# A token table laid out by partitions and read with one load, and both turned blocks of the first expert copied by ScalarE

## The chip, the cores and the metric

The kernel runs on one core of a Trainium2 chip. The metric is the device time of one execution in microseconds. A core has five engines that work side by side, each through its own list of instructions: PE (TensorE, matrix products), DVE (VectorE), ACT (ScalarE), POOL (GpSimd) and SP (SyncE, which here issues transfers only). Sixteen DMA engines move data between DRAM and the on-chip memory. Engines wait for one another and for transfers through semaphores.

## The reference, cut to what matters

Attention over 4 batches, 8 heads and 576 positions of 64 values, with a window in half of the heads and a dilated window in the others. Its result is read as 2304 tokens of 512 values. Each token then goes to one of 8 experts, the one with the largest gate value; an expert takes at most 576 tokens, in order:

```python
logits = x @ w_gate
expert_idx = np.argmax(logits, axis=1)
gate_w = probs[np.arange(N), expert_idx]
for i in range(N):
    e = expert_idx[i]
    if counts[e] < capacity:          # 576
        disp[e, counts[e]] = x[i]
        pos[i] = counts[e]
        counts[e] += 1
        keep[i] = True
h = np.maximum(np.einsum('ecd,edf->ecf', disp, w1), 0.0)
y = np.einsum('ecf,efd->ecd', h, w2)
out[i] = gate_w[i] * y[expert_idx[i], pos[i]]     # for kept tokens
```

## The kernel before, in words

**Attention and routing.** The 2304 tokens go through attention in nine stretches of 256 tokens (two blocks of 128). The kernel's builder holds a small planner (class `Plan`, line 64): every step is an operation with an engine, a duration, a rank and the operations it depends on, and the planner writes them out one by one, in the order in which they could start by its own durations. So each engine's list in this part is the planner's choice. A stretch loads its parts of q, k and v on SP's queue (lines 497 to 528), forms scores on PE, exponentials on ACT, row sums and their reciprocals on DVE (line 671), and multiplies the probabilities by those reciprocals on POOL (line 675: tiles `pr_7p` and so on, d and p for the two kinds of heads); PE transposes the result (line 681) and multiplies by v (line 703).

At the end of a stretch comes routing (`plan_route`, line 908). DVE takes the maximum of the gate values, the expert's number as `idx` (kept as e - 100) and a one-hot matrix; PE adds up ranks with a triangular matrix (line 993); DVE picks each token's rank within its expert, `rk` (line 1011), a large number `over_all` where the rank is 576 or more (line 1017), and the place in the table (lines 1021 and 1025), e * 576 + rank. Each of these is a DVE instruction on a 128 x 2 tile. The stretch's rows go to DRAM as `xrow` (issued by SP, line 848). Two scatters on POOL (line 1049), each with 128 entries of 4 bytes, write token numbers to the places in the DRAM tensor `table`, one 4-byte entry per place. The table starts filled with 2304 (lines 604, 757 and 773); that number stands for no token.

**Early work.** After the sixth stretch (number 5) the first two experts' lists are already partly known. `plan_early` (line 853) loads two blocks of 128 entries of both lists to `early_ix` (two loads, lines 859 to 865, issued by SP at line 863). They wait for that stretch's scatters, and later scatters wait for them. POOL then gathers the rows by those lists, two blocks for expert 0 and one for expert 1 (line 869), and SP's transposing transfers (line 884) turn them. Their products with w1 are among the last steps of attention.

**The experts.** After attention `load_index` (line 1153) brings all eight lists to the tile `ix`: eight loads of 4 x 128 entries (line 1159) and two for the last 64 entries, one for the first expert and one for the other seven (line 1161). Every entry is a 4-byte element of its own in the transfer, as neighbours of a list go to different partitions. POOL gathers the tokens' rows by these lists (line 1176): for the first expert its blocks 1, 2 and 0 in that order. A branch (line 1365) repeats early work where the early lists no longer hold. PE then multiplies expert 0's first block by w2 (`gemm2`, line 1273), and, as that expert's rows beyond the early ones came late, blocks 1 and 2 are turned on PE (`turn`, line 1197: eight 128 x 128 transposes at line 1202 into one bank each). The copy of the turned block from the bank to the tile `xe` alternates: ACT for block 1 (line 1207), DVE for block 2 (line 1205). `load_gate` and `second_gate` (DVE), `drain2` (ACT) and `base1`, the first products with `xe` (PE, line 382), follow. From the third expert on, SP's transfers turn the blocks instead. Weights of all experts come in 512-KB pieces (line 323), are split by ACT and DVE into a high and a low f16 part (`w1h`, `w1l`, `w2h`, `w2l`; lines 345 to 351), and results are scattered to the output by POOL (line 1277).

```python
def c_sl():
    nc.vector.scalar_tensor_tensor(out=small("sl", [128, NBK]), in0=flat("idx"), scalar=float(cap), in1=flat("rk"), ...)
def c_slots():
    nc.vector.scalar_tensor_tensor(out=slots[:, b0:b0 + NBK], in0=t["sl"], scalar=100.0 * cap, in1=over_all[:, b0:b0 + NBK], ...)
```

Of the kernel before, what the change touches and what calls it, by code (L numbers as in the profile page):

```python
# [13 lines left out]
I32 = mybir.dt.int32  # L14
AF = mybir.ActivationFunctionType
ALU = mybir.AluOpType
AX = mybir.AxisListType
# [23 lines left out]
NLIM = 6  # L41
# [163 lines left out]
def shape_constants(B, H, S, E, NT, cap):  # L205

    p = np.arange(128)
    parts = [np.eye(128, dtype=np.float32)]
    parts.append((p[:, None] < p[None, :]).astype(np.float32))
    parts.append(np.tile(np.arange(E, dtype=np.float32) - 100.0, (128, 1)))  # L210
    parts.append((np.arange(NT // 128)[None, :] * 128 + p[:, None]).astype(np.float32))
    for e in range(E):
        lims = form_limits(E, cap, e)
        parts.append(np.tile(np.array(lims + [1e9] * (NLIM - len(lims)), np.float32), (128, 1)))
    parts += unit_masks(B, S)[0]
    return np.ascontiguousarray(np.concatenate(parts, axis=1), np.float32)
# [3 lines left out]
def attention_moe(ctx: ExitStack, tc: tile.TileContext, q, k, v, w_gate, w1, w2, consts, out, cap):  # L220
# [25 lines left out]

    NC0 = 256 + E + NTB + E * NLIM
    con = cpool.tile([128, NC0], F32, name="con")
# [3 lines left out]
    tokid = con[:, 256 + E:256 + E + NTB]  # L252
    limits = con[0:1, 256 + E + NTB:NC0].rearrange("p (e k) -> p e k", e=E)
    tri = cpool.tile([128, 128], F16, name="tri")
# [9 lines left out]
    cnt_i = cpool.tile([1, E + 1], I32, name="cnt_i")  # L264
    nblk = (cap + 127) // 128
    blank = cpool.tile([128, RW], F32, name="blank")
# [5 lines left out]
    xrow = dpool.tile([NT + 1, RW], F32, name="xrow")  # L272
    table = dpool.tile([E * cap, 1], I32, name="table")

# [181 lines left out]
    with ExitStack() as actx:  # L456
# [146 lines left out]

        fill = ap1.tile([128, E * cap // 128], I32, name="fill")
        taken = {"S": 0, "T": 0, "V": 0}
# [247 lines left out]
        def plan_early(sb, at):  # L853
# [4 lines left out]

            def load(e):
                r = table[e * cap:(e + 1) * cap]  # L860
                full = sum(n == 128 for n in n_b)
                if full:
                    nc.sync.dma_start(out=lists[:, e, 0:full], in_=r[0:full * 128].rearrange("(a p) o -> p (a o)", p=128))
                if full < EB:
                    nc.sync.dma_start(out=lists[0:n_b[full], e, full:], in_=r[full * 128:cap])

# [7 lines left out]

            early_ix.extend(dma(lambda e0=e0: load(e0), 0.1, at + 0.6, sent[sb]) for e0 in range(len(EARLY)))
            for e0 in range(len(EARLY)):
# [4 lines left out]
                for j in range((EN[e0] + 127) // 128):  # L881
                    o = add(lambda e, e0=e0, j=j, g=g: fetch(e0, j, g), "POOL", 1.04, [clear, early_ix[e0], rows_out[sb]], at + 0.7, xfer=0.8)
                    n = n_b[j]
# [24 lines left out]
        def plan_route(sb, at):  # L908
# [107 lines left out]
            def c_over():  # L1016
                nc.vector.tensor_scalar(out=over_all[:, b0:b0 + NBK], in0=flat("rk"), scalar1=float(cap), scalar2=float(BIG),
                                        op0=ALU.is_ge, op1=ALU.mult)

            def c_sl():  # L1020
                nc.vector.scalar_tensor_tensor(out=small("sl", [128, NBK]), in0=flat("idx"), scalar=float(cap), in1=flat("rk"),
                                               op0=ALU.mult, op1=ALU.add)

            def c_slots():
                nc.vector.scalar_tensor_tensor(out=slots[:, b0:b0 + NBK], in0=t["sl"], scalar=100.0 * cap, in1=over_all[:, b0:b0 + NBK],
                                               op0=ALU.add, op1=ALU.add)

# [20 lines left out]
            def scatter(blk):  # L1048
                ins = nc.gpsimd.indirect_dma_start(  # L1049
                    out=table, out_offset=bass.IndirectOffsetOnAxis(ap=slots[:, blk:blk + 1], axis=0),  # L1050
                    in_=tok_i[:, blk:blk + 1], in_offset=None, bounds_check=E * cap - 1, oob_is_err=False)
                tc.declare_no_dep(ins.ins, group="dispatch", reason="slots are distinct")
# [7 lines left out]
            idx = dve(c_idx, [cand])  # L1060
            oh = dve(c_oh, [idx])
            rank = add(lambda e: c_rank(), "PE", 0.1, [oh, o_cast] + prev_seen, at + 0.3)
            sums = dve(c_sums, [ex])
# [12 lines left out]
            over = dve(c_over, [rk])  # L1076
            sl = dve(c_sl, [rk])
            slot = dve(c_slots, [over, sl])
            if last:
# [71 lines left out]
    nusual = min(BULK // 128, nblk)  # L1151

    def load_index(e0, e1):

        rows_e = table[e0 * cap:e1 * cap].rearrange("(e s) o -> s e o", s=cap)
        for e in range(e0, e1):
            r = table[e * cap:(e + 1) * cap]
            if nf:
                nc.sync.dma_start(out=ix[:, e, 0:nf], in_=r[0:nf * 128].rearrange("(a p) o -> p (a o)", p=128))
            if e == e0 and cap % 128:  # L1160
                nc.sync.dma_start(out=ix[0:cap % 128, e0:e1, nf], in_=rows_e[nf * 128:cap].rearrange("p e o -> p (e o)"))

# [171 lines left out]

    load_index(0, 1)
    if E > 1:
        load_index(1, E)
    gather(0)
# [43 lines left out]
    for e in range(min(E, len(EARLY))):  # L1382
        for i, j in enumerate(range(EN[e] // 128, nusual)):
            turn(e, j, banks[((3, 5), (6, 7))[e][i % 2]], (nc.scalar, nc.vector)[i % 2])
        if e == 0:
# [64 lines left out]
```

## Time and profile before

| what | us |
|---|---|
| three runs, median (lowest to highest) | 432.93 (431.42 to 433.8) |
| the profiled execution, its own time | 430.79 |
| its span, first to last instruction | 428.9 |
| PE busy | 341.7 (80%) |
| DVE busy | 244.9 (57%) |
| ACT busy | 228.5 (53%) |
| POOL busy | 147.9 (34%) |

The span is cut in 40 slices of 10.7 us; each digit is the busy share of an engine in tenths, PEclk the granted clock of TensorE in tenths of full speed, DMA the mean share in use of 16 engines:

| row | slices |
|---|---|
| PE | 5889957798792987667559899898958959899791 |
| DVE | 6799969997883748112152645643563475765200 |
| PEclk | 9999989999996999669699999999979999989898 |
| DMA | 7996898554798941559815299497695797990000 |

Attention ends near 165 us, in the sixteenth slice; the experts fill the rest. A releaser ("<-") is the instruction whose semaphore ended a wait, inferred from events; where the named engine had long been done, it was another. A stall counts only where the engine that bounds a stretch has to stand still for it.

### The profile page before, as it was taken

The numbers are of one execution on the slowest core, as the hardware profiler recorded it, in microseconds if no ns is written. First come the engines' busy times: TensorE is split into PE (matmuls) and PEld (weight loads), VectorE is DVE, ScalarE is ACT, GpSimd is POOL, SyncE is SP. The second block draws the span as 40 slices with busy tenths as digits, with TensorE's granted clock in tenths as the row PEclk, the third lists the DMA queues.
The fourth block names the chain that finished last, engine by engine and source line by source line (L and its number), as shares of the span: only waits on it lengthen the run. The fifth ranks groups of instructions, "written<-read, shape, count | busy, mean of one in ns | idle before, by whom it ended". The sixth has DMA issues, their size and how long they took to land. (4 is left out here: it accounts for less than half of the span.)

```text
span 428.9 us, 10118 instructions
## 1 busy us (share of the span) xinstructions
PE 341.7 (80%) x3643; PEld 245.7 (57%) x3643; DVE 244.9 (57%) x825; ACT 228.5 (53%) x577; POOL 147.9 (34%) x157
## 2 busy tenths in 40 slices
PE   5889957798792987667559899898958959899791
PEld 3677745475561777257544776774825637687340
DVE  6799969997883748112152645643563475765200
ACT  4888948687781871123161644553464375765210
POOL 6465756757425425532000230310301214110110
PEclk9999989999996999669699999999979989999898
DMA  7996898554798941559815299497695797990000
GB/s 209 252 241 188 166 269 213 134 150 83 87 106 314 156 168 54 101 137 352 111 60 215 85 234 280 157 204 268 215 195 216 243 235 260 174 303 29 29 32 29
DMA packets 83267, 74.59 MB, mean 174 GB/s; under 512 B 48098, under 2 KB 65506, under 8 KB 83187
## 3 DMA queue, kind: packets, MB, share of 16 engines
q1 hardware_dynamic: 78274, 61.23, 58.3%
q0 software_dynamic: 4912, 12.25, 8.2%
q8 instruction: 56, 0.92, 1.1%
q14 instruction: 25, 0.20, 0.2%
HBM read 58.09 MB, written 11.51 MB: 162 GB/s over the span
## 5 line engine op out<-in xcount | busy, mean ns | idle before, releaser
L382 PE MATMUL bank<-xe,w1h 128*128 128x192 f16 (+2 forms) x832 | 95.6, 241 | 18.2 <-issue 7.2
L382 PE MATMUL bank<-xe,w1l 128*128 128x192 f16 (+2 forms) x416 | 92.1, 241 | 0.0
L382 PEld LDWEIGHTS <-w1h 128*128 128x128 f16 x832 | 71.3, 100 | 22.8 <-ACT y L1290 9.5
L1277 POOL DMA_INDIRECT out_dram<-y,ix x26 | 26.5, 1021 | 163.9 <-ACT y L1284 138.6
L1273 PE MATMUL bank<-w2h,hh 128*128 128x512 f16 x120 | 47.9, 399 | 12.0 <-issue 8.9
L351 DVE SCALAR_TENSOR_TENSOR w1l<-wst,w1h 128x1024 f16<-128x1024 f32 x32 | 38.6, 1239 | 29.6 <-ACT w1h L345 28.5
L388 ACT ACTIVATE hh<-bank 128x384 f16<-128x384 f32 (+1 forms) x64 | 27.8, 476 | 40.0 <-PE bank L382 37.3
L389 DVE SCALAR_TENSOR_TENSOR hl<-bank,hh 128x384 f16<-128x384 f32 (+1 forms) x64 | 31.4, 534 | 30.7 <-ACT hh L388 24.1
L1273 PE MATMUL bank<-w2l,hh 128*128 128x512 f16 x120 | 47.9, 399 | 0.0
L1273 PEld LDWEIGHTS <-hh 128*128 128x128 f16 x240 | 23.9, 102 | 41.4 <-issue 16.0
L1273 PE MATMUL bank<-w2h,hl 128*128 128x512 f16 x120 | 47.4, 395 | 0.0
L1284 ACT ACTIVATE y<-bank,gate 64x512 f32<-64x512 f32 (+1 forms) x25 | 17.1, 684 | 55.4 <-PE bank L1273 30.1
L351 DVE SCALAR_TENSOR_TENSOR w2l<-wst,w2h 128x1024 f16<-128x1024 f32 x32 | 37.6, 1218 | 15.3 <-ACT w2h L345 11.2
L382 PEld LDWEIGHTS <-w1l 128*128 128x128 f16 x416 | 41.3, 100 | 0.2
L1291 DVE SCALAR_TENSOR_TENSOR y<-bank,gate,y 64x512 f32<-64x512 f32 x17 | 12.6, 743 | 44.9 <-ACT y L1290 43.4
L1176 POOL DMA_INDIRECT xg<-xrow,ix x26 | 26.3, 1011 | 33.4 <-DVE hl L389 21.0
L345 ACT ACTIVATE w2h<-wst 128x1024 f16<-128x1024 f32 x32 | 32.1, 1047 | 0.7
L1049 POOL DMA_INDIRECT table<-tok_i,slots x18 | 21.8, 1210 | 23.1 <-DVE lost_i L1037 6.6
L1290 ACT ACTIVATE y<-bank,gate 64x512 f32<-64x512 f32 x17 | 11.6, 684 | 31.3 <-PE bank L1273 24.8
L345 ACT ACTIVATE w1h<-wst 128x1024 f16<-128x1024 f32 x26 | 26.1, 1050 | 0.7
L725 DVE TENSOR_TENSOR xT<-bank,xT 128x128 f16<-128x128 f32 (+1 forms) x54 | 20.6, 448 | 4.4 <-ACT xT L535 4.1
L1273 PEld LDWEIGHTS <-hl 128*128 128x128 f16 x120 | 12.3, 102 | 15.7 <-issue 2.8
(350 smaller groups left out, 718.8 us busy)
## 6 DMA issues: line engine op xcount, KB each, us to landing
wst<-in_moe_w_dram SPq DMA_DIRECT2D x64, 512.0 KB
xrow<-row SPq DMA_DIRECT2D x9, 520.0 KB
vp<-in_v_dram SPq DMA_DIRECT2D x32, 96.0 KB
rawpq<-in_q_dram SPq DMA_DIRECT2D x6, 256.0 KB
rawpk<-in_k_dram SPq DMA_DIRECT2D x6, 256.0 KB
vd<-in_v_dram SPq DMA_DIRECT2D x4, 384.0 KB
vd<-in_v_dram SPq DMA_DIRECT2D x2, 320.0 KB
vd<-in_v_dram SPq DMA_DIRECT2D x2, 256.0 KB
```

The lines of the kernel that those rows point to most:

```text
L345: nc.scalar.activation(out=hi, in_=t, func=AF.Copy, scale=SW)
L351: nc.vector.scalar_tensor_tensor(out=lo, in0=t, scalar=SW, in1=hi, op0=ALU.mult, op1=ALU.subtract)
L382: nc.tensor.matmul(out=view(f), lhsT=w[wt][:, c, f * 128:(f + 1) * 128], rhs=x[:, xo + c, a:a + n], start=(kk == 0), stop=(kk == 3 * ND - 1))
L388: nc.scalar.activation(out=hh, in_=p, func=AF.Relu)
L389: nc.vector.scalar_tensor_tensor(out=hl, in0=p, scalar=0.0, in1=hh, op0=ALU.max, op1=ALU.subtract)
L725: nc.vector.tensor_tensor(out=dst, in0=src, in1=hi, op=ALU.subtract)
L1049: ins = nc.gpsimd.indirect_dma_start(out=table, out_offset=bass.IndirectOffsetOnAxis(ap=slots[:, blk:blk + 1], axis=0), in_=tok_i[:, blk:b ...
L1176: nc.gpsimd.indirect_dma_start(out=g[:n, j], out_offset=None, in_=xrow, in_offset=bass.IndirectOffsetOnAxis(ap=ix[:n, e, j:j + 1], axis=0) ...
L1273: nc.tensor.matmul(out=p[:n], lhsT=ht[:, f, j * 128:j * 128 + n], rhs=w[wt][:, f], start=first, stop=final)
L1277: ins = nc.gpsimd.indirect_dma_start(out=out, out_offset=bass.IndirectOffsetOnAxis(ap=ix[:n, e, j:j + 1], axis=0), in_=y[:n], in_offset=No ...
L1284: nc.scalar.activation(out=y[a:n], in_=bank2(e, j)[a:n], func=AF.Copy, scale=gate[a:n, e, j:j + 1])
L1291: nc.vector.scalar_tensor_tensor(out=y[0:m], in0=p[0:m], scalar=gate[0:m, e, j:j + 1], in1=t[0:m], op0=ALU.mult, op1=ALU.add)
```

## The change

It has four parts. The place of a token of rank r at expert e becomes row r mod 128, column e * 5 + r // 128 of a table of 128 rows and 40 columns, so the flat place is r * 40 + e * 5 + r // 128 - (r // 128) * 128 * 40. The number r // 128 is counted on DVE by comparing the rank with 128, 256, 384 and 512 (four new columns of the constants) and summing the ones. Two consecutive ranks of one expert are then 160 bytes apart instead of 4. The early lists of both experts become one load of 256 pieces of two neighbouring entries, the eight main lists one load of 128 rows of 160 bytes. And both turned blocks of expert 0 are copied by ACT; expert 1 keeps one block each for ACT and DVE. The routing of a stretch has four DVE instructions more (first, block, blocks, place), and `slots` is a plain sum.

```diff
+    parts.append(np.tile(128.0 * np.arange(1, (cap + 127) // 128, dtype=np.float32), (128, 1)))
...
-    table = dpool.tile([E * cap, 1], I32, name="table")
+    table = dpool.tile([128 * E * nblk, 1], I32, name="table")
+    by_place = table.rearrange("(p e a) o -> p e (a o)", p=128, e=E)
+    starts = con[:, NC1:NC0]
...
-        fill = ap1.tile([128, E * cap // 128], I32, name="fill")
+        fill = ap1.tile([128, E * nblk], I32, name="fill")
...
-            def load(e):
-                r = table[e * cap:(e + 1) * cap]
-                full = sum(n == 128 for n in n_b)
-                if full:
-                    nc.sync.dma_start(out=lists[:, e, 0:full], in_=r[0:full * 128].rearrange("(a p) o -> p (a o)", p=128))
-                if full < EB:
-                    nc.sync.dma_start(out=lists[0:n_b[full], e, full:], in_=r[full * 128:cap])
+            def load():
+                nc.sync.dma_start(out=lists, in_=by_place[:, 0:len(EARLY), 0:EB])
...
-            early_ix.extend(dma(lambda e0=e0: load(e0), 0.1, at + 0.6, sent[sb]) for e0 in range(len(EARLY)))
+            early_ix.append(dma(load, 0.1, at + 0.6, sent[sb]))
...
-                    o = add(lambda e, e0=e0, j=j, g=g: fetch(e0, j, g), "POOL", 1.04, [clear, early_ix[e0], rows_out[sb]], at + 0.7, xfer=0.8)
+                    o = add(lambda e, e0=e0, j=j, g=g: fetch(e0, j, g), "POOL", 1.04, [clear, early_ix[0], rows_out[sb]], at + 0.7, xfer=0.8)
...
+            def c_first():
+                nc.vector.tensor_scalar(out=small("first", [128, NBK]), in0=flat("idx"), scalar1=100.0, scalar2=float(nblk),
+                                        op0=ALU.add, op1=ALU.mult)
+            def c_block():
+                nc.vector.tensor_tensor(out=small("past", [128, NBK, nblk - 1]), in0=t["rk"].broadcast_to([128, NBK, nblk - 1]),
+                                        in1=starts.rearrange("p (a k) -> p a k", a=1).broadcast_to([128, NBK, nblk - 1]), op=ALU.is_ge)
+            def c_blocks():
+                nc.vector.tensor_reduce(out=small("blk", [128, NBK]), in_=t["past"], axis=AX.X, op=ALU.add)
             def c_sl():
-                nc.vector.scalar_tensor_tensor(out=small("sl", [128, NBK]), in0=flat("idx"), scalar=float(cap), in1=flat("rk"),
+                nc.vector.scalar_tensor_tensor(out=small("sl", [128, NBK]), in0=flat("rk"), scalar=float(E * nblk), in1=t["first"],
                                                op0=ALU.mult, op1=ALU.add)
+            def c_place():
+                nc.vector.scalar_tensor_tensor(out=small("place", [128, NBK]), in0=t["blk"], scalar=1.0 - 128 * E * nblk, in1=t["sl"],
+                                               op0=ALU.mult, op1=ALU.add)
             def c_slots():
-                nc.vector.scalar_tensor_tensor(out=slots[:, b0:b0 + NBK], in0=t["sl"], scalar=100.0 * cap, in1=over_all[:, b0:b0 + NBK],
-                                               op0=ALU.add, op1=ALU.add)
+                nc.vector.tensor_tensor(out=slots[:, b0:b0 + NBK], in0=t["place"], in1=over_all[:, b0:b0 + NBK], op=ALU.add)
...
-            sl = dve(c_sl, [rk])
-            slot = dve(c_slots, [over, sl])
+            blk = dve(c_blocks, [dve(c_block, [rk, o_con])])
+            sl = dve(c_sl, [rk, first])
+            slot = dve(c_slots, [over, dve(c_place, [sl, blk])])
...
-    load_index(0, 1)
-    if E > 1:
-        load_index(1, E)
+    nc.sync.dma_start(out=ix, in_=by_place)
...
-            turn(e, j, banks[((3, 5), (6, 7))[e][i % 2]], (nc.scalar, nc.vector)[i % 2])
+            turn(e, j, banks[((3, 5), (6, 7))[e][i % 2]], nc.scalar if e == 0 else (nc.scalar, nc.vector)[i % 2])
```

## Rows read from the trace of the kernel before

**Rows 1.** The page of the profile, part 1: busy time in us of each engine, its share of the span, and its number of instructions.

```profile
PE 341.7 (80%) x3643; PEld 245.7 (57%) x3643; DVE 244.9 (57%) x825; ACT 228.5 (53%) x577; POOL 147.9 (34%) x157
```

**Rows 2.** What TensorE waited for over the whole run: line waiting, the engine and tile that ended the wait, us in total, times, longest.

```profile
PE bank L681 <- POOL pr_7p L675: 8.5, 1, 8.5
...
PE bank L1273 <- ACT hh L438: 5.7, 1, 5.7
...
PE bank L681 <- POOL pr_3d L675: 4.3, 1, 4.3
PE bank L382 <- DVE xe L1205: 4.2, 1, 4.2
```

**Rows 3.** Busy time in us of each engine (and instructions) in the stretch from 61 to 130 us; then TensorE's granted clock, the share of the DMA engines and the GB/s they moved.

```profile
61.00:130.00 69.00, 56.80 (x767) 41.52 (x764) 62.68 (x347) 54.99 (x210) 38.50 (x40) 0.99 0.67 130
```

**Rows 4.** POOL's timeline between 40 and 186 us: start, duration in us, engine, line, operation, tiles, count; in brackets the idle time before it and what ended it.

```profile
41.51 0.97 POOL L1049 DMA_INDIRECT table<-tok_i,slots  x1 [0.30 <-issue]
...
57.07 1.26 POOL L545 TENSOR_TENSOR pairq<-rawpq,blank 128x512 f32<-128x512 f32 x1 [4.86 <-DVE w1l L351]
...
116.73 0.97 POOL L1049 DMA_INDIRECT table<-tok_i,slots  x1 [0.30 <-PE bank L939]
...
123.27 0.83 POOL L675 TENSOR_TENSOR pr_7d<-pr_7d,su_7d 128x384 f32<-128x384 f32 x1 [2.57 <-ACT pr_7p L655]
132.26 1.29 POOL L869 DMA_INDIRECT early_g<-xrow,early_ix  x1 [8.17 <-DMA early_ix<-table]
133.86 1.77 POOL L869 DMA_INDIRECT early_g<-xrow,early_ix  x1 [0.30 <-DVE mx_8p L647]
135.93 1.00 POOL L869 DMA_INDIRECT early_g<-xrow,early_ix  x1 [0.31 <-issue]
136.96 1.61 POOL L675 TENSOR_TENSOR pr_7p<-pr_7p,su_7p 128x384 f32<-128x384 f32 x2
...
164.35 4.71 POOL L1049 DMA_INDIRECT table<-tok_i,slots  x1 [0.30 <-issue]
175.39 1.04 POOL L1176 DMA_INDIRECT xg<-xrow,ix  x1 [6.33 <-DMA ix<-table]
```

**Rows 5.** What SP's DMA queue waited for over the whole run.

```profile
SPq L1159 <- DMA table<-tok_i,slots: 9.0, 1, 9.0
...
SPq L863 <- DMA table<-tok_i,slots: 4.4, 1, 4.4
```

**Rows 6.** SP's timeline, in stretches around 43, 125 and 172 us: start and duration of the issues of a line, the tiles, and how many issues.

```profile
42.76 3.63 SPq L497 DMA_DIRECT2D rawdk<-in_k_dram  x2
...
119.66 0.93 SPq L528 DMA_DIRECT2D vp<-in_v_dram  x2
125.08 0.90 SPq L863 DMA_DIRECT2D early_ix<-table  x2
126.03 2.44 SPq L323 DMA_DIRECT2D wst<-in_moe_w_dram  x3
...
171.77 0.36 SPq L1159 DMA_DIRECT2D ix<-table  x1
```

**Rows 7.** Stretches of 2 us: busy time in us of each engine (and instructions), TensorE's granted clock, the mean busy share of the DMA engines (over 1 where packets overlap), and GB/s.

```profile
14.00:16.00 2.00, 2.00 (x19) 1.19 (x19) 1.52 (x17) 2.00 (x13) 0.49 (x2) 1.00 0.91 202
42.00:44.00 2.00, 1.94 (x23) 1.45 (x20) 1.97 (x10) 1.40 (x4) 1.99 (x3) 1.00 1.06 84
44.00:46.00 2.00, 1.66 (x18) 1.20 (x16) 2.00 (x11) 2.00 (x10) 1.57 (x3) 1.00 0.53 21
120.00:122.00 2.00, 2.00 (x28) 1.31 (x28) 1.74 (x8) 2.00 (x13) 0.69 (x1) 1.00 1.89 63
122.00:124.00 2.00, 2.00 (x42) 1.51 (x36) 2.00 (x7) 2.00 (x8) 0.73 (x1) 1.00 0.90 15
124.00:126.00 2.00, 1.46 (x30) 1.21 (x28) 2.00 (x16) 0.90 (x5) 0.09 (x1) 1.00 0.47 25
132.00:134.00 2.00, 0.00 (x0) 0.00 (x0) 1.26 (x4) 0.00 (x0) 1.43 (x2) 0.50 1.02 409
134.00:136.00 2.00, 0.00 (x0) 0.00 (x0) 0.74 (x1) 0.00 (x0) 1.69 (x2) 0.50 0.98 388
```

**Rows 8.** VectorE's timeline at 128 us: the first and the last of four small operations that stand next to one another.

```profile
128.35 0.15 DVE L987 RECIPROCAL row<-sums 128x2 f32<-128x2 f32 x1
...
128.57 0.16 DVE L671 RECIPROCAL su_7p<-su_7p 128x4 f32<-128x4 f32 x1
```

**Rows 9.** The one line that holds the branch: its engines' instructions, duration in ns (least, median, most), and the start of the first and last in us.

```profile
L1365 PEldq COMPARE_BRANCH  x1: 5601/5601/5601, 169.2 to 169.2; - x1
```

**Rows 10.** VectorE's timeline at the end of attention and at the first expert's turn.

```profile
162.41 0.15 DVE L1021 SCALAR_TENSOR_TENSOR sl<-idx,rk 128x2 f32<-128x2 f32 x1
162.60 0.16 DVE L1025 SCALAR_TENSOR_TENSOR slots<-sl,over_all 128x2 int32<-128x2 f32 x1
...
186.90 0.69 DVE L1205 COPY xe<-bank 128x1024 f16<-128x1024 f16 x1 [10.08 <-remote]
```

**Rows 11.** TensorE's timeline at the first expert's turn: the transposes, and the first products behind them.

```profile
182.39 1.06 PE L1202 MATMUL bank<-ident,xg 128*128 128x128 f16 x16
187.64 0.50 PE L382 MATMUL bank<-xe,w1h 128*128 128x192 f16 x2 [4.20 <-DVE xe L1205]
```

**Rows 12.** ScalarE's timeline at the same place.

```profile
184.10 1.02 ACT L1207 ACTIVATE xe<-bank 128x1024 f16<-128x1024 f16 x1 [8.11 <-issue]
```

More of the change, by code (lines that the diff above doesn't have):

```diff
@@ L245, in attention_moe @@
     ctx.enter_context(tc.manual_schedule())
-    NC0 = 256 + E + NTB + E * NLIM
+    nblk = (cap + 127) // 128
+    NC1 = 256 + E + NTB + E * NLIM
+    NC0 = NC1 + nblk - 1
     con = cpool.tile([128, NC0], F32, name="con")
@@ L252, in attention_moe @@
     tokid = con[:, 256 + E:256 + E + NTB]
-    limits = con[0:1, 256 + E + NTB:NC0].rearrange("p (e k) -> p e k", e=E)
+    limits = con[0:1, 256 + E + NTB:NC1].rearrange("p (e k) -> p e k", e=E)
     tri = cpool.tile([128, 128], F16, name="tri")
@@ L264, in attention_moe @@
     cnt_i = cpool.tile([1, E + 1], I32, name="cnt_i")
-    nblk = (cap + 127) // 128
     blank = cpool.tile([128, RW], F32, name="blank")
@@ L1050, in scatter @@
                     out=table, out_offset=bass.IndirectOffsetOnAxis(ap=slots[:, blk:blk + 1], axis=0),
-                    in_=tok_i[:, blk:blk + 1], in_offset=None, bounds_check=E * cap - 1, oob_is_err=False)
+                    in_=tok_i[:, blk:blk + 1], in_offset=None, bounds_check=128 * E * nblk - 1, oob_is_err=False)
                 tc.declare_no_dep(ins.ins, group="dispatch", reason="slots are distinct")
@@ L1061, in plan_route @@
             oh = dve(c_oh, [idx])
+            first = dve(c_first, [idx])
             rank = add(lambda e: c_rank(), "PE", 0.1, [oh, o_cast] + prev_seen, at + 0.3)
@@ L1151, in attention_moe @@
     nusual = min(BULK // 128, nblk)
[L1153 to L1161, printed above, removed]
     def late_order(e):
```

## The prediction

> **What bounds the kernel now.** I read the page first. TensorE (PE) leads with 80% of the span, but VectorE (DVE) has 57% and neither share says which of them ends a stretch [rows 1]. So next came PE's waits. Four of them concern this change: 8.5 us for POOL's normalised probabilities pr_7p, 4.3 us for pr_3d, 5.7 us for ACT's hh at line 438, and 4.2 us for the turned block at line 1205 [rows 2]. The third view is busy time by stretch. Between 61 and 130 us DVE is busy 62.68 of 69.00 us and PE only 56.80: there DVE is the bound [rows 3]. Outside of it PE is held by single late arrivals.
>
> The longest arrival is the stop that ends at 137.84. POOL's timeline shows its chain. After 123.27 POOL stands until 132.26, put down to the load of the early lists; then three gathers follow, and only behind them, at 136.96, the normalisation that PE wants [rows 4]. SP's queue shows why the list came late. Its issue had waited 4.4 us for the table scatter [rows 5], went out at 125.08 in two pieces, and three weight loads followed from 126.03 [rows 6].
>
> The fourth view is what the DMA engines moved, in stretches of 2 us. Behind the pair of scatters whose second starts at 116.73 [rows 4] the rate falls to 63, 15 and 25 GB/s, while the engines' busy share goes as high as 1.89: they are occupied and move almost nothing. The same follows the pair whose second starts at 41.51 (84, then 21 GB/s). At 132 to 134 us, where gathers run but no scatter, it is 409. From 14 to 16 us, behind the write that fills the table with 144-byte rows, it is 202 [rows 7]. So the stall comes with the scatters, which write 128 single 4-byte entries each, and not with any write to the table.
>
> **The change part by part.**
>
> *Layout.* A token of rank r now goes to row r mod 128 of a row-per-partition table. Tokens that follow one another in an expert's list lay 4 bytes apart and now lie 160 bytes apart. The number of writes, their size and the 18 POOL instructions stay. What the distance is worth no row shows. One end is nothing, the other the whole of the stalls behind scatters. The first stall: PE stands 8.5 us before 137.84. If the scatters land at once, SP, done with its earlier issues at 120.59 (119.66 + 0.93 [rows 6]), can issue the list then. Taking the 3.6 us from list issue at 171.77 to the gather at 175.39 as landing [rows 4, 6], the gathers begin at 124.3. At the 1.00 us of the third one each, with two gaps of 0.3, they end by 127.9. The reciprocal that pr_7p needs starts at 128.57 [rows 8], so POOL is free in time and after 0.9 us of its normalising (137.84 less 136.96) PE goes on at about 129.6, 8.2 us earlier. DVE used the stop, though: 1.26 us in 132 to 134 and 0.74 in 134 to 136 [rows 7], weight work that must then be done elsewhere by the engine that bounds. I take 6.2.
>
> The second stall: SP's pair of loads at 42.76 took 3.63 us to issue, inside the stall [rows 6]; a pairq on POOL at 57.07 comes after 4.86 us of waiting [rows 4], and PE's wait for pr_3d follows it. The wait is named after DVE, whose own work was finished just then, so a late load is my reading, and I take 2 of its 4.3 us. The third is at attention's end: the last scatter occupies POOL for 4.71 us, and SP waits 9.0 us for it [rows 4, 5]. PE's branch at line 1365 takes 5.6 us [rows 9], and ACT's hh, behind which PE waits 5.7, comes after it. Whether a branch is held up by the DMA stall no row shows: between 0 and 5.6, and I take 1.5, nearer nothing, as it starts 5 us after the last scatter's issue. Together the layout gives 9.7, or nothing.
>
> *Four more DVE instructions in each of nine stretches* (first, block, blocks, place; slots only changes its kind). Small DVE operations that stand among others start 0.07 us apart: the four from 128.35 to 128.57 [rows 8]. For the 28 of the seven stretches that lie before the stop this is 28 x 0.073 = 2.0 us; DVE has 0.91 of its time in use there, so 1.9 count. Bounds are 0 (they fall into DVE's idle tenth) and 36 x 0.08 = 2.9. In the last stretch, where each one waits for the one before, they start 0.19 apart (162.41 to 162.60 [rows 10]). The way from rank to slots gets two links longer, +0.4 on the path, as scatters, lists and gathers all queue behind it.
>
> *The early list as one load* of 256 eight-byte pieces for two of 256 four-byte ones. Its issue shrinks from 0.90 us for both [rows 6] by half, and of the some 6.3 us between issue and gather up to half may go. In the case above it is already contained; without relief it is worth 0 to 3.1, and I take 1.5 (neither end is nearer by a row).
>
> *The main lists as one load* of 128 rows of 160 bytes in place of ten loads. The first goes out at 171.77 in 0.36 us [rows 6]; the nine behind it fall away. POOL's first gather could start perhaps 1.5 us before 175.39. I cost it at nothing: the gathered blocks are turned by PE only at 182.39, behind the pass that starts once hh is there [rows 11], so that pass covers the gathers. If the branch came sooner, the gather would be the next thing late, which is why I gave the third stall only 1.5.
>
> *The turned block.* ACT takes 1.02 us for a copy [rows 12], DVE 0.69 at 186.90 [rows 10]. If PE hands the second block over only then, ACT ends 0.33 later and PE at 187.64 [rows 11] starts as much later. If the block was ready when ACT finished the first at 185.12, ACT would end at 186.14 and not 187.59: 1.4 sooner. DVE did nothing else for 10 us, which speaks for the first; I take 0 between +0.3 and -1.4.
>
> *The filling write* grows from 144 to 160 bytes a row, hidden as it is now by 202 GB/s behind it [rows 7]. The bounds are numbers in instructions that are there anyway, and four more columns ride in the load of the constants, for which nothing in [rows 2] waits.
>
> **The sum.** -6.2 - 2.0 - 1.5 + 1.9 + 0.4 + 0 = -7.4. The profiled execution took 430.79 us, 428.9 of it the span, so it would go to 423.4. It lies 2.1 under the median of 432.93 on which I forecast: 432.93 - 7.4 = 425.5.
>
> **The rivals.** One half per cent, 2.2 us, is about what a measurement of this kernel can tell from no change.
>
> *A, the sum above.* For it speaks that the engines are busy and move nothing, and only where entries lying next to one another are written. Against it: entries of eight experts are mixed already, and a stall that begins 2 to 3 us after a scatter has left POOL might belong to something else that runs then. Its range goes from the whole stalls without the DVE debit (-8.2 - 4.3 - 1.5 + 1.9 + 0.4 - 1.4 = -13.1, 420) to a third of the 9.7 with DVE's additions hidden (-3.2 + 0.4 = -2.8, 430).
>
> *B, the stall is a price of each small write, wherever it goes.* The 256 writes of a pair remain, and so do the stalls; the new layout's only gain is the shorter early list. +1.9 + 0.4 - 1.5 + 0 = +0.8, 433.7, with 431.5 to 435. For it: both layouts write 4 bytes at a time, and the fill, whose rows are 36 times as long, passes without a stall, which fits size as well as distance. The Trainium skill says as much in "DMA: Bandwidth & Descriptors", Specifications: a transfer under 512 B makes the engine read, modify and write. The trace agrees for 4 bytes and not for 144; by that rule alone B would hold.
>
> *C, the slower one.* DVE bounds 61 to 130 and is given 36 more instructions, each a full turn of its queue; no stall goes, and the early list lands when the weight loads queued behind it let it. +2.9 + 0.4 + 0.3 = +3.6, 436.5. It decides as soon as the layout and the list together give less than 1.4 us.
>
> *That the change doesn't do what it says:* the planner may place the longer chain so that the gathers still go ahead of pr_7p. That falls under A when the list is early (it costs nothing then) and under B when it isn't.
>
> **How the numbers follow.** A 0.55, B 0.26, C 0.19. I prefer A because three separate stalls have the same sign (occupied engines, no bytes) and stand behind scatters alone; I keep almost half because nothing in the trace parts distance from count. The predicted time is A's, 425.5, by itself 420 to 430. The range reaches over B to the lower part of C: 421.0 to 435.5; left out are A's best end (0.04) and most of C (0.14). A is faster by over 0.5%, B within it, C slower: 0.55, 0.26, 0.19.
>
> **What would show it.** Right: in 120 to 126 us over 100 GB/s, the list issued by SP near 121, gathers near 124 and no PE wait over 2 us for pr_7p; the rate in 42 to 46 at 150 or more; one load of the main lists near 172 or before. DVE's small operations in 61 to 130 up by 20, its busy time there by 1.5 to 2. For B: 10 to 60 GB/s again behind each pair of scatters, and the gathers' wait only 1 to 3 us shorter. For C: PE's waits for DVE rows in 61 to 130 grow by 2 or more, and the stop at 130 stays. What would make it wrong altogether is a planned order in which other work moves: a wait of PE for a row that isn't in [rows 2].

## The result, and the profile after

The changed kernel took 421.06 us (median; four runs from 418.18 to 425.26) beside 432.46 for the kernel before. The ratio is 0.9713, with an interval of 0.9648 to 0.9777; ratios, here and below, take the undisturbed runs alone, medians all of them. The kernel is faster, as forecast, but by 11.4 us between the medians (12.4 by the ratio) where the sum said 7.4. On the forecast's scale the ratio gives 420.5, just under the range's lower end of 421.0.

The profiled execution after took 421.89 us, its span 420.1. The first view is busy time by stretch (busy us of each engine, granted clock, share of the DMA engines, GB/s), answering [rows 7].

```profile
42.00:44.00 2.00, 1.42 (x19) 0.93 (x18) 2.00 (x8) 1.43 (x3) 1.55 (x2) 1.00 0.76 177
44.00:46.00 2.00, 2.00 (x28) 1.42 (x28) 1.44 (x15) 1.78 (x6) 1.82 (x3) 1.00 1.09 312
120.00:122.00 2.00, 2.00 (x26) 1.67 (x26) 1.39 (x6) 2.00 (x12) 0.00 (x0) 0.50 0.36 87
122.00:124.00 2.00, 2.00 (x23) 1.48 (x20) 1.91 (x11) 1.52 (x8) 0.82 (x1) 0.89 0.94 218
124.00:126.00 2.00, 2.00 (x23) 1.30 (x23) 1.60 (x20) 1.98 (x7) 0.83 (x1) 1.00 0.82 271
```

Where the rate had been 63, 15 and 25 GB/s it is 87, 218 and 271, and from 44 to 46 it is 312 in place of 21. The 87 is no stall: the DMA engines' share is 0.36, so there was little to move, where before it was 1.89 at 63 GB/s. TensorE's granted clock reads 0.50 from 120 to 122, the lower of its two levels, with PE busy all the time; it had been busy for 1.08 and 0.91 us in the two stretches from 112 to 116. So part of the time won there is worked off at 1.2 GHz. What made the clock fall is not shown: in the kernel before PE was busy for 1.10 and 0.64 us in the same two stretches and the clock stayed at 1.00, and it reads 1.00 from 120 to 122 in two of the changed kernel's four profiles.

Next SP's issues and POOL's timeline, answering [rows 4, 6].

```profile
120.95 0.84 SPq L533 DMA_DIRECT2D vp<-in_v_dram  x2
121.88 0.43 SPq L865 DMA_DIRECT2D early_ix<-table  x1
...
169.19 0.33 SPq L1342 DMA_DIRECT2D ix<-table  x1
```

```profile
114.38 0.83 POOL L680 TENSOR_TENSOR pr_6p<-pr_6p,su_6p 128x384 f32<-128x384 f32 x1 [0.41 <-DVE idx L975]
...
118.45 0.97 POOL L1064 DMA_INDIRECT table<-tok_i,slots  x1 [0.30 <-issue]
...
126.48 1.07 POOL L869 DMA_INDIRECT early_g<-xrow,early_ix  x1 [1.31 <-DMA wst<-in_moe_w_dram]
...
129.17 1.00 POOL L869 DMA_INDIRECT early_g<-xrow,early_ix  x1 [0.30 <-issue]
...
132.77 1.24 POOL L680 TENSOR_TENSOR pr_7p<-pr_7p,su_7p 128x384 f32<-128x384 f32 x1 [1.74 <-DVE cand L968]
...
161.97 4.75 POOL L1064 DMA_INDIRECT table<-tok_i,slots  x1 [0.30 <-issue]
173.43 1.04 POOL L1183 DMA_INDIRECT xg<-xrow,ix  x1 [6.71 <-DMA ix<-table]
```

The early list is issued at 121.88, right behind the loads at 120.95, and in this execution no longer waits for a scatter; the first gather is at 126.48 and not 132.26, the normalisation of pr_7p at 132.77 and not 136.96. PE's 8.5 us for pr_7p are gone from its list of waits. These two answer to [rows 2]:

```profile
PE bank L1280 <- ACT hh L443: 3.7, 1, 3.7
PE bank L686 <- ACT kTd L540: 3.7, 1, 3.7
```

The wait for pr_3d (4.3 us) is also gone, but one for kTd, 3.7 us, stands at nearly its place (until 61.92). This is not the relief of the stall. It comes with the planner's other order, as the experiments show: with the layout alone the wait for pr_3d stays, and with the four DVE instructions alone, in the old layout, it is the same wait for kTd. It is the sign that the prediction named for an order in which other work moves, a wait that is not in [rows 2].

What the change added shows on the page (busy time by engine, [rows 1]) and in DVE's last chain ([rows 10]).

```profile
PE 348.2 (83%) x3638; PEld 251.2 (60%) x3638; DVE 252.9 (60%) x855; ACT 231.3 (55%) x583; POOL 149.0 (35%) x157
```

```profile
159.41 0.16 DVE L1011 TENSOR_REDUCE rk<-sel 128x2 f32<-128x16 f32 x1
...
159.68 0.16 DVE L1026 TENSOR_TENSOR past<-rk,con 128x8 f32<-128x8 f32 x1
...
159.87 0.16 DVE L1030 TENSOR_REDUCE blk<-past 128x2 f32<-128x8 f32 x1
160.07 0.16 DVE L1037 SCALAR_TENSOR_TENSOR place<-blk,sl 128x2 f32<-128x2 f32 x1
160.26 0.16 DVE L1041 TENSOR_TENSOR slots<-place,over_all 128x2 int32<-128x2 f32 x1
```

DVE has 252.9 us in place of 244.9, 8.0 more. In the last stretch `past`, `blk`, `place` and `slots` start about 0.2 us apart, as dependent operations do; the way from rank to slots is 0.85 us and was 0.46.

Last the end of attention and the first expert's turn: ACT's timeline, the branch (duration in ns) and PE's, answering [rows 9, 11, 12].

```profile
162.55 0.60 ACT L443 ACTIVATE hh<-bank 128x512 f16<-128x512 f32 x1 [3.81 <-DMA xrow<-row]
...
177.86 1.02 ACT L1214 ACTIVATE xe<-bank 128x1024 f16<-128x1024 f16 x1 [7.11 <-issue]
179.06 1.02 ACT L1214 ACTIVATE xe<-bank 128x1024 f16<-128x1024 f16 x1 [0.18 <-PE bank L1209]
```

```profile
L1370 PEldq COMPARE_BRANCH  x1: 3610/3610/3610, 165.9 to 165.9; - x1
```

```profile
178.40 0.62 PE L1209 MATMUL bank<-ident,xg 128*128 128x128 f16 x8 [0.63 <-DMA xg<-xrow,ix]
180.13 0.24 PE L387 MATMUL bank<-xe,w1h 128*128 128x192 f16 x1 [1.11 <-issue]
```

From the issue of the last rows (159.56) to ACT's hh, the row that waits for them, it is 3.0 us; before, it was 6.3 (162.28 to 168.59). The branch takes 3.6 us and took 5.6. The second copy starts 0.18 us behind the first, and PE's first product with the turned block comes at 180.13, 7.5 us earlier than the 187.64 of before. From there to the end it is 240.0 us in place of 241.3. So of the profile's 8.8 us, 2.7 had been won when the last rows were issued, 4.8 more by that product, and 1.3 after it. The last scatter is no shorter, 4.75 us for 4.71.

### The profile page after: what moved, and what is told of

Read it like the earlier page. It is cut to its first block, busy times and chain, and to the rows that moved or that the text cites. A ratio compares the mean times of both kernels' runs of the same rounds, so it can differ in the third digit from the quotient of the medians.

```text
span 420.1 us, 10128 instructions
## 1 busy us (share of the span) xinstructions
PE 348.2 (83%) x3638; PEld 251.2 (60%) x3638; DVE 252.9 (60%) x855; ACT 231.3 (55%) x583; POOL 149.0 (35%) x157
## 5 line engine op out<-in xcount | busy, mean ns | idle before, releaser
L356 DVE SCALAR_TENSOR_TENSOR w2l<-wst,w2h 128x1024 f16<-128x1024 f32 x32 | 37.6, 1218 | 14.3 <-ACT w2h L350 12.2
L1297 ACT ACTIVATE y<-bank,gate 64x512 f32<-64x512 f32 x17 | 11.6, 684 | 33.7 <-PE bank L1280 26.5
L1064 POOL DMA_INDIRECT table<-tok_i,slots x18 | 22.8, 1269 | 18.1 <-DVE lost_i L1052 5.4
L350 ACT ACTIVATE w1h<-wst 128x1024 f16<-128x1024 f32 x25 | 25.0, 1048 | 0.7
```

Source lines behind the costliest of these rows:

```text
L350: nc.scalar.activation(out=hi, in_=t, func=AF.Copy, scale=SW)
L356: nc.vector.scalar_tensor_tensor(out=lo, in0=t, scalar=SW, in1=hi, op0=ALU.mult, op1=ALU.subtract)
L1064: ins = nc.gpsimd.indirect_dma_start(out=table, out_offset=bass.IndirectOffsetOnAxis(ap=slots[:, blk:blk + 1], axis=0), in_=tok_i[:, blk:b ...
```

## The experiments

They ran in five sittings on several chips, in which the kernel before took 424 to 434 us; each is compared with its sitting's own runs of before. Theory A is the prediction's: entries written close together stall the DMA engines, and distance ends that. Theory B says that each small write has its price wherever it goes, and a third that the loads alone brought the gain.

**Distance alone.** The scale goes into constants, so no instruction is added; the write that fills the table grows sixteenfold with the distance.

```diff
-    table = dpool.tile([E * cap, 1], I32, name="table")
+    table = dpool.tile([E * cap * 16, 1], I32, name="table")
+    entries = table.rearrange("(s w) o -> s (w o)", w=16)[:, 0:1]
...
-    parts.append(np.tile(np.arange(E, dtype=np.float32) - 100.0, (128, 1)))
+    parts.append(np.tile(16 * cap * (np.arange(E, dtype=np.float32) - 100.0), (128, 1)))
...
-                ... in0=flat("idx"), scalar=float(cap), in1=flat("rk"),
+                ... in0=flat("rk"), scalar=16.0, in1=flat("idx"),
```

> The kernel before with one thing changed: neighbours of a list lie 64 bytes apart in the table instead of 4 (the scale is folded into constants, so no instruction is added; lists still come in 4-byte elements by ten loads; the fill grows to 295 KB). If distance ends the stalls (theory A), the two stretches behind a pair of scatters that moved under 30 GB/s move over 150, PE's wait for pr_7p (8.5 us) goes below 2, and the time falls by 5 to 9 us: 424 to 428. If each small write has its price wherever it goes (theory B), the stalls stay at 10 to 60 GB/s and the time stays within 2 us of before. If the gain of the change came from its loads alone, also no change here.

415.44 us beside 423.97, ratio 0.9783 (0.9732 to 0.9833). Its stretches behind scatters, and POOL's timeline:

```profile
44.00:46.00 2.00, 2.00 (x20) 1.48 (x18) 2.00 (x9) 1.45 (x8) 2.00 (x3) 1.00 1.15 245
120.00:122.00 2.00, 2.00 (x33) 1.39 (x30) 2.00 (x8) 2.00 (x12) 0.27 (x1) 1.00 0.97 248
122.00:124.00 2.00, 2.00 (x48) 1.57 (x46) 2.00 (x8) 1.75 (x7) 0.83 (x1) 1.00 1.23 214
124.00:126.00 2.00, 1.34 (x22) 1.07 (x20) 2.00 (x17) 1.14 (x7) 0.21 (x1) 1.00 0.99 358
```

```profile
116.94 0.97 POOL L1050 DMA_INDIRECT table<-tok_i,slots  x1 [0.30 <-ACT pr_7d L656]
...
125.79 1.07 POOL L870 DMA_INDIRECT early_g<-xrow,early_ix  x1 [2.13 <-DMA early_ix<-table]
...
129.50 1.61 POOL L676 TENSOR_TENSOR pr_7p<-pr_7p,su_7p 128x384 f32<-128x384 f32 x2
```

None of these stretches falls under 200 GB/s, the first gather is at 125.79, and pr_7p is normalised at 129.50, against the prediction's 128.7. PE's wait for pr_7p is 1.4 us. The one for pr_3d is still there:

```profile
PE bank L682 <- POOL pr_3d L676: 4.1, 1, 4.1
```

Run twice more, in other sittings:

> The kernel before with entries 64 bytes apart, run again so that it stands beside the other three on one chip. As before: 0.978 (0.973 to 0.983). It carries the size of the layout's gain; if it falls within 0.5% of the changed kernel, the change's loads, DVE instructions and copy together are worth nothing.

> Entries 64 bytes apart and nothing else, beside the next one: 0.967 to 0.978 as on the other chips.

420.29 beside 434.14 (0.9666, 0.9606 to 0.9726) and 419.72 beside 432.2 (0.9715, 0.9682 to 0.9748). B falls: the number and the size of the scatters' writes are those of before. So does the third theory: this one has the old loads.

**Nearer together.** As above with 4 in place of 16, so 16 bytes.

> The kernel before with list neighbours 16 bytes apart in place of 4. The changed kernel has about three of a scatter's entries in each 64 bytes, this one four, the kernel before sixteen. If it is the number of a scatter's entries that fall close together that stalls, this is nearly as good as 64 bytes apart: 0.978 to 0.985, rates behind scatters over 100 GB/s. If any two neighbours within 64 bytes are enough, the stalls stay (10 to 60 GB/s for 4 to 6 us) and the time is 0.995 to 1.0 of before.

419.76 beside 431.96, 0.9743 (0.9685 to 0.98). The rates behind its pair of scatters:

```profile
114.00:116.00 2.00, 2.00 (x29) 1.43 (x25) 1.71 (x13) 2.00 (x11) 0.83 (x1) 1.00 0.93 268
116.00:118.00 2.00, 1.99 (x43) 1.56 (x43) 2.00 (x9) 2.00 (x13) 0.00 (x0) 1.00 0.96 247
118.00:120.00 2.00, 2.00 (x44) 1.66 (x38) 2.00 (x9) 1.29 (x3) 0.83 (x1) 1.00 1.18 256
```

So neighbours within 64 bytes are no harm by themselves; that what counts is how many of a scatter's entries fall close together fits all that is seen here.

**DVE's instructions alone**, in the kernel before: the four operations of the diff, with factors that leave the places as they were.

```diff
+            first = dve(c_first, [idx])
...
-            sl = dve(c_sl, [rk])
-            slot = dve(c_slots, [over, sl])
+            blk = dve(c_blocks, [dve(c_block, [rk, o_con])])
+            sl = dve(c_sl, [rk, first])
+            slot = dve(c_slots, [over, dve(c_place, [sl, blk])])
```

> The kernel before with the change's four more DVE instructions in each stretch and its longer chain to the slots, the places and loads as before. Theory of the prediction: +1.9 for the 28 instructions in the stretch that DVE bounds and +0.4 for the last chain, 434.5 to 436. Rival: they fall into DVE's idle tenth and the stop at 130 takes them in, 0 to +0.5. A third: the planner, which counts each at 0.08, moves other work, and the time goes by more than 3 either way.

423.59 beside 423.97, 0.995 (0.9912 to 0.9988). The prediction's +2.3 us is not there. Most of the stalls are: in the rate from 118 to 120 us, behind the pair of scatters whose second starts at 117.30, and in the early list, which waits 6.7 us for a scatter and is issued by SP at 125.88. In the two stretches after 124 the rate is as low, but the engines' share is 0.10 and 0.13, so there little was in flight.

```profile
44.00:46.00 2.00, 1.87 (x28) 1.58 (x30) 2.00 (x19) 1.63 (x4) 1.69 (x3) 1.00 0.92 262
118.00:120.00 2.00, 2.00 (x23) 1.15 (x19) 1.86 (x11) 1.70 (x9) 0.61 (x2) 1.00 0.96 27
124.00:126.00 2.00, 2.00 (x46) 1.56 (x40) 1.61 (x13) 2.00 (x11) 0.00 (x0) 1.00 0.10 22
126.00:128.00 2.00, 1.38 (x15) 0.82 (x14) 2.00 (x26) 2.00 (x9) 0.00 (x0) 1.00 0.13 18
```

```profile
PE bank L684 <- ACT kTd L538: 3.7, 1, 3.7
```

```profile
125.88 0.38 SPq L866 DMA_DIRECT2D early_ix<-table  x1
```

The planner's order did change: in this one the scatters come at 55, 78, 89 and 110 us, as in the changed kernel, where before they came at 59, 73, 96 and 104. With that order the rate from 44 to 46 is 262 GB/s in the old layout, where before it was 21, and PE waits for kTd and no longer for pr_3d. So the rival, that the stalls cover the additions, fits, but a gain from the other order that hides their price fits too; this run does not part the two.

**Both together**: 64 bytes and the four instructions.

> The kernel before with entries 64 bytes apart and with the change's four more DVE instructions in each stretch: the layout's effect and the instructions' (with the order that the planner makes of them) at once, without the one-load lists and without the ACT copy. If the two add up: 0.978 - 0.005 = 0.973. If, with the stalls gone, DVE's instructions are paid for (the prediction's +2.3 us): 0.983. Against the changed kernel the difference is what loads and copy are worth: theory A says under 2 us.

> The same with the change's four more DVE instructions a stretch, again, beside the one without them. The difference of the two is the price of these instructions and of the order that the planner makes with them when no stall covers it: 0.5% (+2.3 us) by the prediction, 1% by the runs on two chips (0.989 against 0.978). If the runs on two chips misled: none.

427.06 beside 431.96 (0.9886, 0.9838 to 0.9933), and, beside the variant without the instructions in one sitting, 425.79 against 420.29 (0.9835 against 0.9666). They do not add up: without stalls the instructions cost 5.5 us by these medians and 7.3 by the ratios, not the prediction's 2.3. Two causes were left, their own time or the planner's other order. So they were emitted together with operations that the planner had anyway; the order of all that was there before is then unchanged on every engine.

```diff
-            over = dve(c_over, [rk])
-            sl = dve(c_sl, [rk])
-            slot = dve(c_slots, [over, sl])
+            over = dve(lambda: (c_over(), c_block()), [rk])
+            sl = dve(lambda: (c_sl(), c_blocks()), [rk])
+            slot = dve(lambda: (c_place(), c_slots()), [over, sl])
```

> Entries 64 bytes apart and the four more DVE instructions a stretch, but each of them emitted together with an operation that the planner had already: its order on every engine is that of the kernel before, with 36 DVE instructions more. If the 5.5 us are DVE's time: 425.8 as without this (0.983 of before). If they come from the planner's other order: near the variant without the instructions, 420.3 to 422.5 (0.967 to 0.973), 0 to 2.3 us for the instructions.

> The same with the 36 DVE instructions and the order of the kernel before on all engines. If the price is DVE's own time: 1 to 1.7% above the one without them. If it is the planner's order: within 0.5%.

427.5 beside 430.74 (0.9872, 0.9791 to 0.9954), and in one sitting 426.89 against 419.72 for the variant without them: 0.9809 (0.9761 to 0.9858) against 0.9715 (0.9682 to 0.9748), 4.1 us. So it is the instructions and not the order alone; whether by DVE's time or by the longer way to the slots, these two do not part. The pages of the two (busy time by engine), first without and then with:

```profile
PE 343.3 (82%) x3643; PEld 247.0 (59%) x3643; DVE 245.4 (59%) x825; ACT 228.8 (55%) x577; POOL 148.6 (36%) x157
```

```profile
PE 347.0 (81%) x3643; PEld 248.0 (58%) x3643; DVE 251.7 (59%) x861; ACT 229.1 (54%) x577; POOL 148.9 (35%) x157
```

DVE has 6.3 us more for 36 instructions, 0.175 each. The changed kernel with its instructions emitted in the same way gains nothing either:

> The changed kernel with its four DVE instructions emitted in the same way, so that the planner's order is nearly that of the kernel before (its one early load is still one operation for two). If the order is what costs, this is the best so far: 417 to 419 (0.960 to 0.966). If DVE's time is what costs: 421, as the changed kernel (0.971).

422.73 beside 430.74, 0.9801 (0.9737 to 0.9866), against 0.9784 for the changed kernel there.

**The changed kernel again**, beside the others.

> The changed kernel itself, beside the others on one chip, as the chip of the first experiments ran the kernel before 2% sooner. If its gain is the same share on every chip: 0.971 of before. If the two variants that lack only the one load (0.985) or only the ACT copy (0.985) tell its size there, as theory A has it with those parts worth nothing: 0.98 to 0.985. If both parts were worth a per cent each: 0.97.

> The changed kernel again, beside the variant that has its distance and its DVE instructions but neither its loads nor its ACT copy. Measured 0.971 and 0.979 so far. The difference to that variant is what the loads are worth: nothing by the prediction, 1% (4 us) by the runs so far. PE's first product with the turned block comes 20.4 us after the issue of the last rows in this one and 21.7 in the other, by their first profiles.

> The changed kernel beside the three others on their chip: 0.971, as on two chips of three.

0.9787 (0.971 to 0.9864), 0.9714 (0.9666 to 0.9761) and 0.9784 (0.9735 to 0.9834). Twice it stood beside the variant with distance and instructions but the old loads and copy: 424.45 against 427.06 and 421.3 against 425.79. Between the medians loads and copy are worth 2.6 and 4.5 us; in the first of the two sittings the intervals overlap.

**Which of them?** The early load in two halves (one load for each expert), the main lists in ten loads of 4-byte elements, and DVE back for one copy:

```diff
-                nc.sync.dma_start(out=lists, in_=by_place[:, 0:len(EARLY), 0:EB])
+                [nc.sync.dma_start(out=lists[:, e], in_=by_place[:, e, 0:EB]) for e in range(len(EARLY))]
```

> The changed kernel with its early load as two loads of 128 eight-byte pieces, one for each expert, issued one behind the other. If the one early load is worth something, the first early gather comes later by about the second issue and landing, 0.5 to 2 us, and the time is 0.5 to 2 us above the changed kernel's (0.971): 0.973 to 0.976. If the number of loads is worth nothing there: 0.971.

422.84 beside 430.74, 0.9818 (0.9762 to 0.9874), where the changed kernel had 0.9784: 2.3 us between the medians, with intervals that overlap.

```diff
-    nc.sync.dma_start(out=ix, in_=by_place)
+    by_list = by_place.rearrange("p e a -> p a e")
+    for e in range(E):
+        nc.sync.dma_start(out=ix[:, 0:4, e:e + 1], in_=by_list[:, 0:4, e:e + 1])
+        if e < 2:
+            es = slice(0, 1) if e == 0 else slice(1, E)
+            nc.sync.dma_start(out=ix[:, 4, es], in_=by_list[:, 4, es])
```

> The changed kernel with its one load of the main lists undone: ten loads again, in elements of 4 bytes (the tile of the lists is turned so that neighbours don't join; the table's layout stays). If the loads of the later lists kept the first expert's gathered rows from landing (theory after the two traces: PE's transposes waited for them until 186.9 before, and no longer after), PE's first product with the turned block comes 2 to 5 us later than in the changed kernel and the time is 2 to 4 us longer, 423 to 425. If the prediction's zero for this part is right, 421 within 1 us.

> The changed kernel with the copies of the first expert's turned blocks as before, ACT for one and DVE for the other. In the changed kernel ACT ends the first copy at 178.88 and begins the second at 179.06 after PE's transposes, so DVE's faster copy should end 0.3 us sooner: 420.7, not to be told from no change. Rival: ACT in series costs or gives 1 us or more, as PE hands on what it wrote sooner to one engine than to the other: 419.5 or 422.5.

0.9851 (0.9795 to 0.9908) and 0.985 (0.98 to 0.99), in one sitting without the changed kernel beside them, so neither has a price of its own. The theory behind the first is not borne out: PE's first product with the turned block comes 21.3 us after the issue of the last rows, in the changed kernel 20.1 to 23.3 over its four profiles. The copy in the kernel before:

> The kernel before with one thing changed: both turned blocks of the first expert copied by ACT. The prediction's bounds are +0.3 and -1.4 us. Where the gathered block only lands when DVE took it, as the trace of before has it, ACT is 0.3 us later and the time stays: 1.000, not to be told from no change. If ACT can take it sooner: 0.997.

432.97 beside 431.96, 0.9977 (0.9934 to 1.002): not to be told from nothing.

**A version of its own**: rows by rank, no arithmetic added, loads of 8 and 32 bytes.

```diff
+    table = dpool.tile([128 * nblk * 16, 1], I32, name="table")
+    by_rank = table.rearrange("(a p w) o -> p a (w o)", p=128, w=16)
...
+                ... in0=flat("rk"), scalar=16.0, in1=flat("idx"), ...        # rank * 16 + expert
...
+                nc.sync.dma_start(out=lists, in_=by_rank[:, 0:EB, 0:len(EARLY)])
...
+    nc.sync.dma_start(out=ix, in_=by_rank[:, :, 0:E])
```

> A version of its own from what is known: the table by rank, 64 bytes to a rank with the eight experts' entries side by side in it. The place is rank x 16 + expert, with no DVE instruction more than in the kernel before and its order; both lists of the early work come with one load of 8-byte pieces, the main lists with one load of 32-byte pieces; the copy stays ACT and DVE. Eight entries of a scatter then share 64 bytes, between the sixteen that stall and the four that don't. If eight are few enough: 0.970, better than the changed kernel (the layout's gain without DVE's price, and the loads). If eight still stall: half of the gain, 0.985, and 20 to 60 GB/s behind scatters for 2 to 4 us.

419.2 us beside 434.14, 0.9673 (0.9627 to 0.9719). There the changed kernel had 421.3: 2.1 us more between the medians, with intervals that overlap. The variant with distance alone had 420.29 (0.9666) there, so in this kernel the fewer loads add nothing that can be told from noise. Up to eight entries in 64 bytes don't stall:

```profile
118.00:120.00 2.00, 2.00 (x42) 1.65 (x40) 1.17 (x11) 2.00 (x10) 1.27 (x2) 1.00 0.62 220
120.00:122.00 2.00, 1.99 (x34) 1.39 (x29) 2.00 (x8) 2.00 (x12) 0.24 (x1) 1.00 0.95 229
122.00:124.00 2.00, 2.00 (x48) 1.58 (x46) 2.00 (x9) 1.74 (x6) 0.83 (x1) 1.00 1.23 226
```

## Why the prediction was right and wrong

**Right: the mechanism.** A was the likeliest, and the layout alone shows it: 8.5, 13.9 and 12.5 us between the medians of three sittings. The steps of the first stall came nearly as worked out. The list went out at 120.57 for a predicted 120.59; it took 5.2 us and not 3.6 to the first gather (125.79 for 124.3), and the normalisation came at 129.50 for 128.7. B fails. By the rule that the prediction drew from the Trainium skill's "DMA: Bandwidth & Descriptors", Specifications, under which transfers below 512 bytes are read, modified and written, the time would have stayed. The writes of 4 bytes remained, and the stall went: the measurement decides that size by itself isn't what stalled here.

**Wrong: the layout's term, too small.** It was put at 9.7 and measured at 11.6 in the mean of the three. The step that failed is the debit of 2.0 us for DVE's weight work inside the first stop. From the start of the second scatter in front of that stop (116.73) to the issue of the last rows (162.28) the one profile of the kernel before takes 45.6 us, the three profiles with the layout alone 37.6 to 37.9. That is 7.7 to 8.0 less, nearly the 8.2 without the debit, where the sum took 6.2. The second stall's 2.0 is right in two of the three: that scatter comes 2.2 and 2.1 us earlier (114.55 and 114.64), with 2.0 and 2.2 us left of the wait for pr_3d, and in the third 0.2 later (116.94), with 4.1 left. The third stall was put at 1.5; from the last rows' issue to PE's first product with the turned block it is 20.6 to 23.2 us in the three and was 25.4, so 2.2 to 4.7. The branch has a part in that: 3.6 to 3.8 us in the three for 5.6 before. The last scatter has none: it still takes 4.70 us, and SP still waits 7.5 to 9.2 us for it.

**Wrong: DVE's four instructions, too cheap.** They were priced at the 0.073 us of independent operations that stand next to one another [rows 8], 1.9 us in all, although the prediction itself called them a chain and priced the last one at 0.19 each [rows 10]. Every stretch has that chain: 0.175 x 36 = 6.3 us of DVE; by the ratios 4.1 us of time with the order held and 7.3 with the planner's other order. That the sum treats terms as independent may have been wrong as well: in the kernel with stalls the same instructions show no price, but there the order had changed with them.

**Wrong: the loads at nothing.** They and the copy give 2.6 to 4.5 us back in the changed kernel. The early list, which the prediction counted as contained in the layout's case, may be half of it (2.3 us between medians, with overlapping intervals); how the rest divides between main lists and copy stays open, since the two variants did not run beside the changed kernel. That gathers are hidden behind the pass on PE was nearly right where the profile shows it (gather at 173.43, transposes from 177.16, with 0.63 us of waiting for the second block's rows). The turned block's wait changes from execution to execution with the same copies: 0.8, 3.2 and 3.9 us in the three profiles with the layout alone.

So the parts, by medians, are -11.6 for distance, +5.5 for DVE and -3.6 for loads and copy, -9.7, beside -11.4, -7.5, -12.8 and -10.2 in the four measurements of the whole. The forecast's errors had opposite signs, so that the total came nearer than its terms is luck; their rest put the time just under the range.

**The slower rival** C had the sign of DVE's part right, and its size (2.9 + 0.4) still too small; that the layout's gain is about twice that part decides the case.

## What to carry to other kernels

When DMA engines are busy and move nothing, look at which small writes are in flight and how close together they land; spreading them may cost only a constant in the address. Price an added instruction by the row of its own kind of neighbour, dependent or not, in the engine that bounds the stretch, and do not take the price that it shows beside stalls for the price without them. Where a planner writes the order, hold the order still before pricing an addition: here it moved other work by itself. Arithmetic on addresses can often be saved by choosing a layout in which the place is linear in what is known.

## What the runs showed of the hardware

The layouts differ in how many of a scatter's 128 entries of 4 bytes lie in 64 bytes. With about sixteen, the kernel before, the DMA engines move 15 to 84 GB/s for about 6 us behind each of the two pairs of scatters looked at here (42 to 48 and 120 to 126 us). With up to eight, four or one it is 181 GB/s or more behind the same two pairs. Not every pair stalls so at once: with the DVE instructions alone, in the old layout, the stretches from 44 to 48 have 262 and 275 GB/s, and the rate falls to 64 only from 50 to 52.

What takes long is not the scatters' own packets. In the packet records of the traces these have 32 bytes and take 13 to 15 ns in the median in every layout. The packets of other transfers do take long. Between 40 and 136 us those over 1 us add up to 240 us in the kernel before, most of them of 1024 and 2080 bytes, and to 229 and 162 us in its two variants with the old layout. In the seventeen profiles with the entries spread it is 6 to 63 us. PE's branch goes the same way: 5.6, 5.5 and 5.0 us in the three with the old layout, 3.3 to 4.1 in the others. What inside the memory does that, no run here shows.

Some of the added DVE instructions also wait on POOL, inside their own row. One of the nine `first`, 0.16 us by itself:

```profile
114.41 0.82 DVE L1022 TENSOR_SCALAR first<-idx 128x2 f32<-128x2 f32 x1
```

It ends at 115.23, 0.67 us over its usual time; POOL's pr_6p, in POOL's timeline above, runs from 114.38 to 115.21. The Trainium skill's "SBUF — State Buffer", section "SBUF: two separate sides", says that DVE and POOL share a pair of ports that one instruction holds to its end while the other waits, where the DVE instruction uses both ports for one input or has two inputs in that memory. The rows agree as far as the end of the wait goes; in which way this instruction read, no row shows. Seven such rows of the six operations from `first` to `slots` take over 0.4 us in that execution, 4.5 us together above 0.15 each, and each ends within 0.02 us of the end of a POOL operation. In the variant that keeps the old order the means of these operations are 0.155 to 0.224 us, so there this is only a small part of DVE's price.
